# Moving the ReLU tiles by 128 bytes in SBUF, and storing the last two output blocks in halves from two queues

## Chip, cores and metric

The kernel runs on one core of one Trainium2 chip. The metric is the device time of one launch in microseconds; the number that stands for a kernel is the median over its runs.

## The reference

A gated linear attention recurrence is followed by a mixture of four dense experts. Per batch (4) and head (8), over 768 steps of width 48:

```python
state = alpha[:, :, t, :, None] * state + np.einsum('bhd,bhe->bhde', k[:, :, t], v[:, :, t])
y[:, :, t] = np.einsum('bhd,bhde->bhe', q[:, :, t], state)
```

The heads are laid side by side, so that x has 3072 rows of 384. Then, with p the row-normalised domain probabilities, four experts of hidden width 1024:

```python
h = np.maximum(x @ w1[e], 0.0)
out += p[:, e:e + 1] * (h @ w2[e])
```

All inputs and the output are float32.

## The kernel before, in words

**Blocks and groups.** The 3072 rows are 24 blocks of 128 rows, ordered by chunk of the sequence and then by batch. They form seven groups: the first two blocks, then five groups of four, then the last two blocks (`groups`, line 113; `LAST` is the number of the last group). The attention of a block is a generator that is advanced in small steps between matmuls of an earlier group's experts (`advance`, line 728), by due times worked out in `deal` (line 697). The order of the instructions on each engine is the order in which the program issues them; nothing reorders them.

**Tasks.** A task is one expert for one group. Groups before the last two take the four experts in turn. The last two groups go through the experts together: for each expert first group `LAST - 1` (four blocks), then group `LAST` (two blocks) (line 116).

**The two matmul stages.** `up` (line 518) computes the hidden values, eight chunks of 128 for up to 512 rows. From the second group on it does so in three products of split operands (lines 553 to 559), two into the PSUM tile `one` and one into `two`. ScalarE and VectorE then join them in the work tile `t` (lines 568 and 570), ScalarE writes the ReLU (line 595), and VectorE writes two more parts of it (lines 597 and 603). These three parts are the tiles called `hT`: four buffers of 12,288 bytes per partition in the pool `hid`. `down` (line 610) multiplies them by w2: at line 650 an `hT` block of 128 x 128 is the stationary operand (the weight load, LDWEIGHTS, engine PEld), and 384 columns of w2 are the moving operand. While the first groups run, the `hT` buffers are also where w2 is landed by DMA (line 217) and, at the start, the inputs of the second block.

**The output.** `add_up` (line 667) adds a finished PSUM sum to the block's accumulator on VectorE (line 679). The accumulator is the tile `acc` of the pool `hid`, also four buffers; in the last group it is a work tile, `QT`. After the last expert a store of the block's 128 rows of 384 (192 KB) is put on a list (line 686). The list is issued in the next `up`, at the end of its second chunk, and once more at the very end of the program. Stores of the last two groups go on SyncE's queue, all others on GpSimd's.

**Memory.** Pools take space in SBUF in the order in which they are opened, and tiles within a pool in the order of their first use. In the pool `work` the tile `x_raw` (line 455, 6,144 bytes per partition) comes last, and the pool `hid` follows it. In the program before, `x_raw` starts at byte 165,856 of each partition, the four `hT` buffers at 172,000, 184,288, 196,576 and 208,864, and the four `acc` buffers at 221,152 and on. The tiles `t` and `QT` lie before `x_raw`, and the pool with the weights before the whole pool `work`.

Of the kernel before, what the change touches and what calls it, by code (L numbers as in the profile page):

```python
# [10 lines left out]
F32 = mybir.dt.float32  # L11
# [9 lines left out]
def kernel(  # L21
# [37 lines left out]
    nc = tc.nc  # L59
# [3 lines left out]
    P = 128  # L63
# [5 lines left out]
    KC = DM // P  # L69
    FCH = F // P  # L70
    NT = B * P
# [6 lines left out]
    assert DM % P == 0 and F % (P * NQ) == 0 and DM <= 512 and KC * QF == FPQ * DM  # L78
    FINE = 1 + 1 / 4096
    TRIM = 1 - 1 / 8192  # L80

    j = np.arange(P)[:, None] % HALF
    n = np.arange(QUAD)[None, :]
# [7 lines left out]
    work = ctx.enter_context(tc.tile_pool(name="work", bufs=2))  # L91
# [22 lines left out]
    LAST = len(groups) - 1  # L114
# [20 lines left out]
    xraws = {}  # L135
# [4 lines left out]
    stores = deque()  # L140
# [80 lines left out]
    def split_piece(l, i):  # L221
# [3 lines left out]

        nc.scalar.activation(out=top, in_=whole, func=ACT.Copy, scale=TRIM)
        yield
        nc.scalar.activation(out=dif, in_=whole, func=ACT.Copy, scale=TRIM * 4096)
        yield
# [43 lines left out]
    def attention(u):  # L273
# [140 lines left out]
        for s in range(2):  # L414
            rows = slice(HALF * s, HALF * (s + 1))
            nc.scalar.copy(out=parts[:HALF, :, s, :, HALF:], in_=far[rows])
        yield
        for s in range(2):
            rows = slice(HALF * s, HALF * (s + 1))
# [9 lines left out]
        def result():  # L429
            yps = ps.tile([P, KC, P], F32, name="yps", tag="w")  # L430
            for c in range(KC):


                if c < 2:
                    now = [[(2 * c + j // 2, j % 2, (0, HD + TAIL)[j % 2], 2 * QUAD * (j % 2))
                            for j in range(4)]]
                    turns = ([(True, now[0])] if cb > 0 else []) + [(False, now[0])]
                else:
                    turns = [(True, [(p, 0, 0, QUAD) for p in range(NP)])] if cb > 0 else []
                    turns += [(False, [(p, i, QUAD + TAIL * i, 0) for p in range(NP)]) for i in range(2)]  # L440
                for n, (past, turn) in enumerate(turns):
                    for j, (p, i, in_v, in_st) in enumerate(turn):
                        nc.tensor.matmul(  # L443
                            yps[QUAD * j:QUAD * (j + 1), c, :],
                            lhsT=flat_st[:, p, in_st:in_st + QUAD] if past
                            else flat_v[:, p, in_v:in_v + QUAD],
                            rhs=QT[:, p, :] if past else lat[:, 2 * p + i, :],
                            start=(n == 0), stop=(n == len(turns) - 1))
            gi, slot = place[cb, b]
            if slot == 0:  # L450
                if gi == 0:
                    xTs[gi] = work.tile([P, 3, KC, NT], F32R, name="xT", bufs=1)
                    xraws[gi] = xTs[gi][:, 2].bitcast(F32)
                elif gi < LAST:
                    xraws[gi] = work.tile([P, KC, NT], F32, name="x_raw", bufs=1)
                else:
                    xraws[gi] = []
            if gi < LAST:
                nc.scalar.copy(out=xraws[gi][:, :, slot * P:(slot + 1) * P], in_=yps)
            else:  # L460

                xraws[gi].append(AT)
                nc.scalar.copy(out=AT[:, :KC, :], in_=yps)
# [6 lines left out]
        for step in (turn_keys, result) if u >= half else (result, turn_keys):  # L470
            step()
            yield

        if cb < NCB - 1:
# [5 lines left out]
            for i in range(2):  # L480
                rows = slice(HD * i, HD * (i + 1))
# [17 lines left out]
    def split_x(gi, step):  # L499
# [7 lines left out]
        for kc in range(KC) if step == 0 else [step - 1]:  # L507
# [3 lines left out]
            for x, out in pieces:  # L511
                if step == 0:
                    nc.scalar.activation(out=out[0], in_=x, func=ACT.Copy, scale=TRIM)
                else:
# [78 lines left out]
    def hidden_parts(x, parts):  # L593
        top, low, dif = parts
        nc.scalar.activation(out=top, in_=x, func=ACT.Relu, scale=TRIM)  # L595
        yield
# [13 lines left out]
    def down(gi, e, slots, between):  # L610
# [20 lines left out]
        for n, (side, slot, part, fc) in enumerate(steps):  # L631
            c, f = divmod(fc, FPQ)
            advance(cost(1, gi, e) * len(slots) / len(steps))
            while between and n >= between[0][0] * len(steps):
                between.popleft()[1]()
            if n and n % (len(steps) // (2 * len(slots))) == 0:
                background()
            if later and n % (len(steps) // 12 - 1) == len(steps) // 12 - 2:
                make_dif(*later.popleft())
            at = (side, slot)  # L640
            if n == begins[at]:
                sums[at] = ps.tile([P, DM], F32, name="ops", tag="g", bufs=4)
            h = hidden[c][:, :, f, slot * P:(slot + 1) * P]
            if part < 3:
                w = wt[1][first + c].rearrange("p t (c d) -> p t c d", d=DM)[:, part, f]
                h = h[:, part]
            else:
                w = wt[1][first + c].rearrange("p (c d) -> p c d", d=DM)[:, f]
                h = h[:, 2].bitcast(F32)
            nc.tensor.matmul(sums[at], lhsT=h, rhs=w, start=(n == begins[at]), stop=(n == ends[at]))  # L650
            if n == ends[at]:
                add_up(gi, e, slot, side, sums.pop(at))
# [14 lines left out]
    def add_up(gi, e, slot, kind, part):  # L667

        cb, b = groups[gi][slot]
        at = b * NCB + cb  # L670
        if e == 0 and (kind == 0 or not split2(gi, e)):
            accs[cb, b] = hid.tile([P, DM], F32, name="acc", bufs=B) if gi < LAST else \
                work.tile([P, NP * P], F32, name="QT")[:, :DM]
        acc = accs[cb, b]
        scale = (p_fine if kind == 0 else p_all)[:, at, e:e + 1]
        if e == 0 and (kind == 0 or not split2(gi, e)):
            nc.scalar.activation(out=acc, in_=part, func=ACT.Copy, scale=scale)
        else:
            nc.vector.scalar_tensor_tensor(out=acc, in0=part, scalar=scale, in1=acc,  # L679
                                           op0=ALU.mult, op1=ALU.add)  # L680
        if kind == 0:
            return
        if e == E - 1:
            del accs[cb, b]
            row = b * S + cb * P
            stores.append(lambda: (nc.sync if gi >= LAST - 1 else nc.gpsimd).dma_start(
                out=out[row:row + P, :], in_=acc))

# [140 lines left out]
```

## Time and profile before

| what | value |
|---|---|
| median of 6 runs | 1057.86 us |
| lowest and highest run | 1057.08 and 1059.69 us |
| the profiled execution: time | 1059.09 us |
| the profiled execution: span from first to last instruction | 1057.3 us |
| TensorE clock granted | 1.000 over the span |
| DMA: mean rate | 238 GB/s, 251.66 MB |
| stores `out_dram<-acc` from GpSimd's queue | 18 of 192 KB, 6.9 us to landing (median) |
| stores `out_dram<-acc` from SyncE's queue | 4 of 192 KB |
| stores `out_dram<-QT` from SyncE's queue | 2 of 192 KB |

The profile is of one execution. PE is TensorE's matrix multiplication and PEld its weight loads, which overlap it; DVE is VectorE, ACT ScalarE, POOL GpSimd, SP SyncE; a q behind a name means the engine's instruction queue, where DMAs are issued and semaphores waited for. Matmul ends are modelled, so the busy time of one matmul overlaps that of the next; the pace of matmuls is better read from their starts. L650 is line 650 of the kernel.

### The profile page before, as it was taken

The numbers are of one execution on the slowest core, as the hardware profiler recorded it, in microseconds if no ns is written. First come the engines' busy times: TensorE is split into PE (matmuls) and PEld (weight loads), VectorE is DVE, ScalarE is ACT, GpSimd is POOL, SyncE is SP. The second block draws the span as 40 slices with busy tenths as digits, with TensorE's granted clock in tenths as the row PEclk, the third lists the DMA queues.
The fourth block names the chain that finished last, engine by engine and source line by source line (L and its number), as shares of the span: only waits on it lengthen the run. The fifth ranks groups of instructions, "written<-read, shape, count | busy, mean of one in ns | idle before, by whom it ended". The sixth has DMA issues, their size and how long they took to land.

```text
span 1057.3 us, 21578 instructions
## 1 busy us (share of the span) xinstructions
PE 1038.0 (98%) x8498; PEld 903.5 (85%) x8498; DVE 781.7 (74%) x1620; ACT 565.7 (53%) x1195; POOL 35.6 (3%) x77
## 2 busy tenths in 40 slices
PE   8899999999999999999999999999999999999998
PEld 8777777687887899898898898998989989898988
DVE  5578777668779778778877777986877875656565
ACT  4687876575665654545546436555474443323232
POOL 3000010000001000000000000000000000000000
PEclk9999999999999999999999999999999999999999
DMA  7596799997878956757759559586594454444531
GB/s 116 163 340 214 233 305 352 323 338 239 278 265 298 370 195 233 315 169 280 284 176 344 224 174 348 180 287 242 168 372 179 184 210 167 192 183 176 206 153 46
DMA packets 158837, 251.66 MB, mean 238 GB/s; under 512 B 120112, under 2 KB 135344, under 8 KB 136208
## 3 DMA queue, kind: packets, MB, share of 16 engines
q1 hardware_dynamic: 152688, 208.87, 57.8%
q0 software_dynamic: 5760, 41.29, 9.7%
q8 instruction: 67, 1.10, 0.4%
q14 instruction: 34, 0.28, 0.1%
q10 hardware_dynamic: 288, 0.12, 0.1%
HBM read 207.79 MB, written 42.47 MB: 237 GB/s over the span
## 4 chain that ended last, share of the span: by engine, by line
PE 83%; ACT 4%; DVE 4%; DMA 4%; SPq 3%; issue 1%; POOL 0%; ACTq 0%; DVEq 0%; POOLq 0%
PE ops L650 35%; PE one L557 23%; PE two L557 11%; PE sc L348 5%; PE yps L443 3%; PE tp L270 3%; PE one L549 1%; ACT qb L321 1%; SPq L214 1%; PE sps L478 1%; PE far L403 1%; DMA w<-kept 1%; DMA kept<-w 1%; DMA w<-in_moe_w_dram 1%; SPq L215 1%
## 5 line engine op out<-in xcount | busy, mean ns | idle before, releaser
L650 PE MATMUL ops<-w,hT 128*128 128x384 f32 x1872 | 346.9, 340 | 0.2 <-DVE hT L603 0.2
L650 PEld LDWEIGHTS ops<-w,hT 128*128 128x128 f32 x1872 | 324.9, 188 | 4.7 <-ACT t L568 0.6
L557 PE MATMUL one<-xT,w 128*128 128x512 f32 x960 | 252.8, 399 | 1.9 <-DMA w<-kept 1.1
L557 PEld LDWEIGHTS one<-xT,w 128*128 128x128 f32 x960 | 175.7, 188 | 40.6 <-DVE dot L292 1.7
L568 ACT ACTIVATE t<-one 128x512 f32<-128x512 f32 (+1 forms) x192 | 107.1, 558 | 176.2 <-PE one L557 170.9
L321 ACT COPY qb<-QT 64x256 f32<-64x256 f32 x336 | 136.6, 407 | 74.5 <-DVE QT L300 40.9
L597 DVE SCALAR_TENSOR_TENSOR hT<-t,hT 128x512 fp32r<-128x512 f32 (+1 forms) x172 | 110.5, 643 | 68.2 <-ACT hT L595 65.8
L570 DVE TENSOR_TENSOR t<-t,two 128x512 f32<-128x512 f32 (+1 forms) x172 | 109.4, 636 | 57.8 <-ACT t L568 29.1
L595 ACT ACTIVATE hT<-t 128x512 fp32r<-128x512 f32 (+1 forms) x172 | 101.8, 592 | 85.7 <-DVE t L570 84.7
L557 PE MATMUL two<-xT,w 128*128 128x512 f32 x480 | 136.3, 392 | 0.0
L557 PEld LDWEIGHTS two<-xT,w 128*128 128x128 f32 x480 | 90.1, 188 | 20.1 <-DVE acc L679 0.3
L603 DVE SCALAR_TENSOR_TENSOR hT<-hT 128x512 fp32r<-128x512 f32 (+1 forms) x172 | 100.9, 634 | 0.0
L650 PE MATMUL ops<-hT 128*128 128x384 f32 x288 | 100.6, 491 | 0.0
L358 DVE COPY_PREDICATED near<-masks,sc 128x256 f32<-128x256 uint8 x144 | 77.0, 534 | 19.3 <-PE sc L348 16.3
L328 DVE TENSOR_TENSOR QT<-QT,dec 128x256 f32<-128x256 f32 x144 | 61.1, 424 | 35.5 <-ACT qb L321 34.8
L348 PEld LDWEIGHTS sc<-qb,KT 128*64 128x64 f32 x2304 | 72.7, 138 | 9.3 <-issue 4.7
L348 PE MATMUL sc<-qb,KT 128*64 128x64 f32 x2304 | 77.2, 223 | 2.6 <-ACT qb L321 2.6
L650 PEld LDWEIGHTS ops<-hT 128*128 128x128 f32 x288 | 52.1, 190 | 29.0 <-issue 0.4
L679 DVE SCALAR_TENSOR_TENSOR acc<-ops,p_all,acc 128x384 f32<-128x384 f32 x82 | 49.9, 614 | 29.5 <-PE ops L650 28.4
L341 DVE TENSOR_TENSOR KT<-KT,dec 128x256 f32<-128x256 f32 x144 | 60.1, 417 | 0.0
L340 ACT COPY KT<-KT 128x256 f32<-128x256 f32 x138 | 57.5, 416 | 3.0
L549 PE MATMUL one<-xT,w 128*128 128x256 f32 (+1 forms) x240 | 46.8, 341 | 1.8 <-DMA w<-in_moe_w_dram 1.2
(90 smaller groups left out, 933.5 us busy)
## 6 DMA issues: line engine op xcount, KB each, us to landing
w<-kept SPq DMA_DIRECT2D x144, 1152.0 KB
kept<-w POOLq DMA_DIRECT2D x32, 1152.0 KB, 7.7
hT<-in_moe_w_dram SPq DMA_DIRECT2D x32, 384.0 KB
w<-in_moe_w_dram SPq DMA_DIRECT2D x48, 128.0 KB
ra<-in_alpha_dram SPq DMA_DIRECT2D x23, 192.0 KB
rk<-in_k_dram SPq DMA_DIRECT2D x23, 192.0 KB
rq<-in_q_dram SPq DMA_DIRECT2D x23, 192.0 KB
out_dram<-acc POOLq DMA_DIRECT2D x18, 192.0 KB, 6.9
```

Source lines behind the costliest of these rows:

```text
L321: nc.scalar.copy(out=qb[rows, :, i, :].rearrange("p a (b r) -> p a b r", r=m), in_=qv[rows])
L328: nc.vector.tensor_mul(qv, qv, spread(dv[:, :, :, 0], m))
L341: nc.vector.tensor_mul(new[:, :, :, 0, :], old[:, :, :, 0, :], spread(halved(decs[li])[:, :, :, 1], m))
L348: nc.tensor.matmul(out[HALF * s:HALF * (s + 1), 2 * p:2 * p + 2, :], lhsT=KTs[li][:, p, HALF * s:HALF * (s + 1)], rhs=qbs[li][:, p, :, QUA ...
L358: nc.vector.copy_predicated(near.rearrange("p a (b two r) -> p a b two r", two=2, r=m)[:, :, :, 1, :], mk.unsqueeze(1).broadcast_to([P, H, ...
L557: nc.tensor.matmul(out, lhsT=w[:, part, kc], rhs=x_part(gi, part, kc), start=(part == terms[0] and kc == 0), stop=(part == terms[-1] and k ...
L568: nc.scalar.activation(out=t, in_=one, func=ACT.Copy, scale=FINE)
L570: nc.vector.tensor_add(t, t, two)
L595: nc.scalar.activation(out=top, in_=x, func=ACT.Relu, scale=TRIM)
L597: nc.vector.scalar_tensor_tensor(out=low, in0=x, scalar=0.0, in1=top.bitcast(F32), op0=ALU.max, op1=ALU.subtract)
L603: nc.vector.scalar_tensor_tensor(out=dif, in0=top.bitcast(F32), scalar=1 / 4096.0, in1=low.bitcast(F32), op0=ALU.mult, op1=ALU.subtract)
L650: nc.tensor.matmul(sums[at], lhsT=h, rhs=w, start=(n == begins[at]), stop=(n == ends[at]))
```

## The change

Three things are edited. A tile of 32 more floats per partition is allocated for `x_raw`, and only its first 1,536 floats are used; with this, everything in the pool `hid`, that is the `hT` and `acc` buffers, starts 128 bytes further on. The stores of group `LAST - 1` go on GpSimd's queue, as those of the groups before do. The stores of group `LAST` are split into rows 0 to 63 on SyncE's queue and rows 64 to 127 on ScalarE's.

```diff
+    PAD = 32
...
                 elif gi < LAST:
-                    xraws[gi] = work.tile([P, KC, NT], F32, name="x_raw", bufs=1)
+                    xraws[gi] = work.tile([P, KC * NT + PAD], F32, name="x_raw", bufs=1)[:, :KC * NT]
+                    xraws[gi] = xraws[gi].rearrange("p (c n) -> p c n", n=NT)
...
         if e == E - 1:
             del accs[cb, b]
             row = b * S + cb * P
-            stores.append(lambda: (nc.sync if gi >= LAST - 1 else nc.gpsimd).dma_start(
-                out=out[row:row + P, :], in_=acc))
+            queues = (nc.sync, nc.scalar) if gi == LAST else (nc.gpsimd,)
+            for i, queue in enumerate(queues):
+                rows = slice(P // len(queues) * i, P // len(queues) * (i + 1))
+                stores.append(lambda queue=queue, rows=rows: queue.dma_start(
+                    out=out[row:row + P, :][rows], in_=acc[rows]))
```

## The prediction

> **What bounds the kernel now.** I read the page's first part and then the busy time by stage.
>
> ```profile
> span 1057.3 us, 21578 instructions
> ...
> PE 1038.0 (98%) x8498; PEld 903.5 (85%) x8498; DVE 781.7 (74%) x1620; ACT 565.7 (53%) x1195; POOL 35.6 (3%) x77
> ...
> 0.00:60.00 60.00, 52.95 (x600) 45.46 (x602) 35.61 (x89) 36.38 (x86) 10.46 (x30) 1.00 0.73 167
> 60.00:165.00 105.00, 97.59 (x967) 74.97 (x962) 84.32 (x187) 78.69 (x175) 6.93 (x13) 1.00 0.83 276
> 165.00:600.00 435.00, 434.38 (x3512) 369.86 (x3512) 334.99 (x683) 248.83 (x513) 13.94 (x26) 1.00 0.76 271
> 600.00:860.00 260.00, 259.62 (x2323) 231.73 (x2322) 205.94 (x426) 137.96 (x294) 4.31 (x8) 1.00 0.69 248
> 860.00:1036.00 176.00, 176.00 (x991) 164.68 (x990) 109.03 (x209) 57.50 (x116) 0.00 (x0) 1.00 0.43 168
> 1036.00:1057.30 21.30, 17.45 (x120) 16.80 (x119) 11.82 (x29) 6.30 (x16) 0.00 (x0) 1.00 0.11 38
> ```
>
> The stage rows give length, then busy time (and count) of PE, PEld, DVE, ACT and POOL, then clock, DMA share and GB/s. From 165 us to 1036 us PE is busy for 870.0 of 871 us. All its waits after 165 us are these, 2.2 us together:
>
> ```profile
> PE one L557 <- DMA w<-kept: 1.1, 1, 1.1
> PE one L557 <- DVE xT L252: 0.5, 1, 0.5
> PE one L557 <- ACT t L568: 0.4, 1, 0.4
> PE ops L650 <- DVE hT L603: 0.2, 1, 0.2
> ```
>
> So in this stretch only two things change the time: how much matmul work there is, which the edit leaves alone, and the distance from one matmul to the next. I looked at that distance next, because the moved `hT` tiles are the stationary operand of L650. The last expert stages of group `LAST - 1` are four equal stretches of 96 matmuls (start, length):
>
> ```profile
> 866.36 17.12 PE L650 MATMUL ops<-w,hT 128*128 128x384 f32 x96
> ...
> 917.25 16.81 PE L650 MATMUL ops<-w,hT 128*128 128x384 f32 x96
> ...
> 967.84 16.81 PE L650 MATMUL ops<-w,hT 128*128 128x384 f32 x96
> ...
> 1018.88 17.12 PE L650 MATMUL ops<-w,hT 128*128 128x384 f32 x96
> ```
>
> Less the last matmul's own 0.34 us (335 ns, the median of L650), over 95 distances, that is 16.78/95 = 176.6 ns in two of them and 16.47/95 = 173.4 ns in the other two. The program has a slow and a fast pace for the same work on the same buffers. Over the whole trace the 1,730 directly following pairs of L650 that are under 250 ns apart have a mean of 174.7 ns.
>
> **The change, part by part.** *The 128 bytes.* No instruction is added or removed. Moved are `hT` and `acc`. What touches them: L650's 2,160 weight loads, L595, L597 and L603 (172 each), L679, the DMAs that land w2 in `hT`, and the stores of `acc`. First, the engines off PE. The rows that allow a comparison are VectorE's at 512 elements: L597 with both inputs in SBUF takes 694 ns, L603 with both in `hT` 683 ns, L570 with one input in PSUM and nothing in `hT` 685 ns. If a better place of `hT` took L597 down to L603, DVE would gain 11 ns x 140 = 1.5 us; if a worse place did the same the other way to both, it would lose 3.1 us. DVE is 74% busy and PE waited for `hT` 0.2 us after 165 us, so either sits beside PE's work; without that cover it would cost those 1.5 or 3.1 us. L595 (632 ns) is the same as L607 (632 ns), which works in place in `hT`, so there is no ACT penalty for either start.
>
> Second, PE. L650's matmuls start on average 174.7 ns apart with 384 columns. L557, whose stationary operand is w1 and not `hT`, is 120 ns apart with 256 columns and 229 ns with 512, which puts 384 columns at 174.5 ns. A load of `hT` therefore costs the pace nothing today. It also has room: L557 shows a load every 120 ns, L650 needs one every 174. Sorting L650's pairs by which quarter of a 2,048-byte row of `hT` the block begins in, the medians are 174, 174, 175 and 174 ns, and no trend. All four of these starts are 480 bytes past a multiple of 512, though, and after the change all are 96 past one, so this trace cannot show the new place itself. I bound it by the two paces: all 1,872 at 173.4 ns gives (174.7 - 173.4) x 1,872 = -2.4 us; all at 176.6 ns gives +3.6 us. I take 0, because slow and fast stretches read the very same addresses, so something other than the place of `hT` picks the pace. The DMAs that land w2 in `hT` (32 of 384 KB) are issued ahead of use; the largest single PE wait on any DMA after 165 us is the 1.1 us above, on weights that do not move. Bounds 0 and 1.1 us, taken 0.
>
> *Group LAST - 1's four stores, SP to POOL.* On SP they are issued at 1032.44 to 1036.68 us and behind them stand only the two last stores. On POOL nothing is queued at that time (no POOL work after 860 us). The price is in these rows (min/median/max ns, first and last start):
>
> ```profile
> L686 POOL DMA_DIRECT2D out_dram<-acc x18: 539/542/547, 167.6 to 850.4; - x18
> ...
> L686 SPq DMA_DIRECT2D out_dram<-acc x4: 332/334/337, 1032.4 to 1036.7; - x4
> ...
> L826 POOLq DRAIN  x3: 40/93/11434, 850.4 to 1057.1; - x3
> ```
>
> Each issue takes 0.54 instead of 0.33 us. The last is issued at 1036.68, over at 1037.2, and landed 9.3 us later at worst (the maximum of the 18), at 1046.5. POOL's closing drain, 11.4 us after its last store in this trace, would end near 1048.7. The program's end collects the engines at 1056.5 us, so 7.8 us of cover remain: cost 0.
>
> *The last group's stores in halves.* The first block's store (1052.75) lies under the second block's matmuls. The second sets the end: accumulator ready 1054.11, issue at 1054.14 for 0.33 us, first packet 1054.97, last packet over at 1055.64, last landing 1055.99, end of span 1057.32. That is 0.03 + 0.33 + 0.50 + 0.67 + 0.35 + 1.33 = 3.2 us. Only two terms can move. The issue becomes two at once, the one on ACT by its rows (0.39 and 0.45 us at the program's start) up to 0.12 us longer than SP's 0.33; ACT's last work ended at 1047.0, so nothing is behind it but its drain. The 0.67 us of packets for 144 packets become two times 72: -0.33 us if they run side by side without hindrance, 0 if they share the same rate. Bounds -0.34 and +0.12 us. I take -0.1, the middle. The Trainium skill speaks against a gain: "DMA: Bandwidth & Descriptors", section "Rules for kernel authors", says that two transfers to disjoint partition halves serialize on the same engines and one 128-partition transfer is to be used. By that rule the packets stay at 0.67 us and the part costs 0.06 to 0.12 us instead of winning 0.1; no row of this trace has two half stores at once.
>
> **Sum.** 0 + 0 - 0.1 us. Against the profiled execution: 1059.09 - 0.1 = 1059.0 us (span 1057.3 to 1057.2, and 1.8 us around it). The median of the runs is 1.2 us below that execution, so 1057.86 - 0.1 = 1057.8 us.
>
> **The rivals.** *A, the new place holds PE at the fast pace (faster).* For it: two paces exist, and L650 has 1,872 matmuls. Against: they occur on the same addresses. Price -2.4 us, and -0.1 from the tail: 1055.4 us. Should the pace carry over into L557 (mean 229.7, best stretches 229.0 ns, 1,440 matmuls) another -0.9: 1054.4 us.
>
> *B, the new place holds PE at the slow pace (slower).* The weight load of `hT` now meets the moving read of w2 in a worse phase. It decides as soon as the mean distance grows by 1 ns: 1,872 x 1 ns = 1.9 us, about the smallest difference that counts; at 176.6 ns it is +3.6 - 0.1: 1061.4 us. For and against as in A.
>
> *C, GpSimd closes late (slower).* If a POOL store or the drain behind it took longer than 1056.5 - 1037.2 = 19.3 us, each us more would lengthen the end by one. At twice the 11.4 us seen, 1037.2 + 22.9 = 1060.1, +3.5 us: 1061.3 us. The DMA share there is 0.11 against 0.69 in the stage where 11.4 us were seen, so I think it most unlikely.
>
> *D, the place does not change* because `hid` does not follow `x_raw`: then only the tail is left, the forecast's own time.
>
> **How the numbers follow.** Forecast, with D: 0.50. A: 0.26. B: 0.22. C: 0.02. A difference counts from 0.2% on (2.1 us), about what a measurement of this kernel can tell from no change: its six runs spread over 2.6 us. A counts as faster, B and C as slower. So faster 0.26, same 0.50, slower 0.24. The forecast's own range is 1057.8 with the tail's and the DMA's bounds and the runs' scatter, 1056.6 to 1059.5 us. As A and B hold nearly half, the range reaches to both: 1054.4 (A with L557) to 1062.0 us (B with half a us of scatter).
>
> **What would show it.** L650's pairs at a mean of 174.7 ns again, stretches of both 16.81 and 17.12 us: the place does nothing. All stretches alike: A or B. L597 and L603 other than 694 and 683 ns: the place matters to VectorE. The end: two issues near the accumulator's last write, packets over in less than 0.67 us, and 3.1 us from there to the end of the span. POOL's drain over by 1050 us: C is out. The prediction is wrong if PE's busy time between 165 and 1036 us changes by over 2 us with the same number of matmuls.

## The result, and the profile after

| | before | after |
|---|---|---|
| median | 1058.05 us (36 runs) | 1055.52 us (16 runs) |
| lowest and highest run | 1056.64 and 1061.71 us | 1054.42 and 1060.00 us |
| the profiled execution: time and span | 1059.09 and 1057.3 us | 1054.98 and 1053.2 us |
| ratio of the times, 95% interval | | 0.9976 [0.9970, 0.9983] |

The kernel became 0.24% faster, 2.5 us. That is the place and the size of rival A (1055.4 us), not of the forecast (1057.8 us). In the changed file some lines stand further down: L650 is now L653, L557 is L560, L597 is L600, L603 is L606, L679 is L682, L686 is L693, L826 is L833. They shift in the other kernels too; the text keeps to L650 and L557.

The page of the kernel after, and its busy time by stage (columns as before: length; PE, PEld, DVE, ACT, POOL with counts; clock, DMA share, GB/s):

```profile
span 1053.2 us, 21582 instructions
...
PE 1035.7 (98%) x8498; PEld 901.6 (86%) x8498; DVE 781.5 (74%) x1620; ACT 565.3 (54%) x1195; POOL 37.8 (4%) x81
...
165.00:600.00 435.00, 434.32 (x3517) 369.69 (x3516) 335.97 (x684) 249.81 (x516) 13.94 (x26) 1.00 0.77 271
600.00:860.00 260.00, 259.62 (x2325) 231.54 (x2325) 205.88 (x426) 137.30 (x292) 4.30 (x8) 1.00 0.69 247
860.00:1036.00 176.00, 176.00 (x1013) 165.53 (x1012) 109.30 (x212) 57.89 (x119) 2.17 (x4) 1.00 0.42 166
```

PE is as busy as before, 869.9 of 871 us, with the same 8,498 matmuls and the same clock. What differs is how many matmuls fit: 1,013 instead of 991 in the last of these stages. Part of the 22 is that the stage begins earlier in the work, so it is the pace that has to be read. The four equal stretches of 96 matmuls, from the timeline of PE (start, length):

```profile
863.07 16.80 PE L653 MATMUL ops<-w,hT 128*128 128x384 f32 x96
...
913.67 16.80 PE L653 MATMUL ops<-w,hT 128*128 128x384 f32 x96
...
964.26 16.80 PE L653 MATMUL ops<-w,hT 128*128 128x384 f32 x96
...
1014.85 16.80 PE L653 MATMUL ops<-w,hT 128*128 128x384 f32 x96
```

Before, two of the four took 17.12 us; now none does. (16.80 - 0.34)/95 is 173.3 ns from start to start. Over the 1,730 directly following pairs the mean fell from 174.74 to 173.27 ns. All waits of PE after 165 us are 1.1 us together, all for the same releasers as before; of before's list only the 1.1 us for a DMA is missing:

```profile
PE one L560 <- DVE xT L254: 0.5, 1, 0.5
PE one L560 <- ACT t L571: 0.4, 1, 0.4
PE ops L653 <- DVE hT L606: 0.2, 1, 0.2
```

**Where the time went.** The two traces hold the same 8,498 matmuls in the same order, so each start can be set against its counterpart. The span is 4.1 us shorter (1057.3 - 1053.2), more than the medians differ, because the profiled execution of before was 1.0 us above its median and that of after 0.5 us below its own. The 4.1 us are:

| part | after less before |
|---|---|
| waits and small differences up to 175 us | -1.6 us |
| L650's pairs: -1.11 us in 165 to 600, -0.64 in 600 to 860, -0.82 later | -2.57 us |
| L557's pairs | about -0.4 us |
| the steps from one line to another after 175 us | +0.2 us |
| from the last accumulator write to the end | +0.2 us |

The first row does not belong to the edit: three kernels below whose times equal before's (`e2`, `e4`, `e5`) show 1.0 to 1.3 us of it too. Without it, -2.57 - 0.4 + 0.2 + 0.2 = -2.6 us stand beside the 2.5 us of the medians. The share of L557 need not belong to the edit either: `e4`, whose operands stand to each other as before's do, has -0.3 us of it in the same stretch after 1,000 us.

### The profile page after: what moved, and what is told of

The parts are those of the page before. It is cut to its first block, busy times and chain, and to the rows that moved or that the text cites. A ratio compares the mean times of both kernels' runs of the same rounds, so it can differ in the third digit from the quotient of the medians.

```text
span 1053.2 us, 21582 instructions
## 1 busy us (share of the span) xinstructions
PE 1035.7 (98%) x8498; PEld 901.6 (86%) x8498; DVE 781.5 (74%) x1620; ACT 565.3 (54%) x1195; POOL 37.8 (4%) x81
## 4 chain that ended last, share of the span: by engine, by line
PE 86%; DVE 4%; ACT 4%; DMA 3%; SPq 1%; issue 1%; POOL 0%; ACTq 0%; DVEq 0%; POOLq 0%
PE ops L653 36%; PE one L560 23%; PE two L560 11%; PE sc L350 6%; PE yps L445 3%; PE tp L272 3%; DMA hT<-in_moe_w_dram 2%; PE one L552 1%; ACT qb L323 1%; PE sps L481 1%; PE far L405 1%; SPq L216 1%; DMA w<-in_moe_w_dram 1%; DVE w L232 1%; DVE near L360 1%
## 5 line engine op out<-in xcount | busy, mean ns | idle before, releaser
L653 PE MATMUL ops<-w,hT 128*128 128x384 f32 x1872 | 344.4, 340 | 0.2 <-DVE hT L606 0.2
L653 PEld LDWEIGHTS ops<-w,hT 128*128 128x128 f32 x1872 | 322.5, 188 | 4.7 <-ACT t L571 0.6
L560 PE MATMUL one<-xT,w 128*128 128x512 f32 x960 | 252.4, 398 | 0.9 <-DVE xT L254 0.5
L560 PEld LDWEIGHTS one<-xT,w 128*128 128x128 f32 x960 | 175.7, 188 | 39.2 <-ACT t L571 1.4
L600 DVE SCALAR_TENSOR_TENSOR hT<-t,hT 128x512 fp32r<-128x512 f32 (+1 forms) x172 | 110.5, 643 | 68.0 <-ACT hT L598 65.9
L560 PE MATMUL two<-xT,w 128*128 128x512 f32 x480 | 136.2, 392 | 0.0
L560 PEld LDWEIGHTS two<-xT,w 128*128 128x128 f32 x480 | 90.0, 188 | 20.1 <-DVE acc L682 0.6
L653 PE MATMUL ops<-hT 128*128 128x384 f32 x288 | 100.9, 491 | 0.5 <-DMA hT<-in_moe_w_dram 0.5
L606 DVE SCALAR_TENSOR_TENSOR hT<-hT 128x512 fp32r<-128x512 f32 (+1 forms) x172 | 100.9, 634 | 0.0
L653 PEld LDWEIGHTS ops<-hT 128*128 128x128 f32 x288 | 52.1, 190 | 29.8 <-DMA hT<-in_moe_w_dram 1.1
L682 DVE SCALAR_TENSOR_TENSOR acc<-ops,p_all,acc 128x384 f32<-128x384 f32 x82 | 49.8, 614 | 28.7 <-PE ops L653 27.7
```

The lines of the kernel that those rows point to most:

```text
L560: nc.tensor.matmul(out, lhsT=w[:, part, kc], rhs=x_part(gi, part, kc), start=(part == terms[0] and kc == 0), stop=(part == terms[-1] and k ...
L600: nc.vector.scalar_tensor_tensor(out=low, in0=x, scalar=0.0, in1=top.bitcast(F32), op0=ALU.max, op1=ALU.subtract)
L606: nc.vector.scalar_tensor_tensor(out=dif, in0=top.bitcast(F32), scalar=1 / 4096.0, in1=low.bitcast(F32), op0=ALU.mult, op1=ALU.subtract)
```

## The experiments

The theory (T) after the result: the weight load of `hT` and the moving read of w2 go on at the same time, and the pace depends on how the two addresses stand to each other. I count this as the **distance**: the byte address of the stationary operand less that of the moving one, modulo 256. It is 64 for L650 before and 192 after; L557 (stationary w1, moving `xT`) has 192 in both. Rivals: the stores made it (S); the place of `hT` by itself counts, whatever w2's is (P); any other place of `hT` would do (O). In the diffs, 32 floats are 128 bytes.

**1. Each part alone, and two other ways to move.** `e1_pad_only` has the 128 bytes and the old stores, `e2_stores_only` the new stores and the old place. `e4_pad_256B` moves `hT` by 256 bytes, so the distance is again 64. `e5_all_moved` moves everything behind the tile `ident`, weights too: `hT` lies at the addresses of `e1`, and the distance is still 64.

```diff
e1, e4 (with + 64):
-                    xraws[gi] = work.tile([P, KC, NT], F32, name="x_raw", bufs=1)
+                    xraws[gi] = work.tile([P, KC * NT + 32], F32, name="x_raw", bufs=1)[:, :KC * NT]
+                    xraws[gi] = xraws[gi].rearrange("p (c n) -> p c n", n=NT)
e5:
-    ident_all = const.tile([P, P + HALF], F32, name="ident")
+    ident_all = const.tile([P, P + HALF + 32], F32, name="ident")[:, :P + HALF]
```

> The 128 bytes alone, all stores as before. If the place of hT holds L650 at its fast pace: mean distance of directly following L650 matmuls 173.3 ns (after: 173.3, before: 174.7), ratio to before 0.9975 or a little lower, as the tail is 0.2 us shorter than in the changed kernel. If the gain came from the stores: 174.7 ns and ratio 1.000. If the pace is a matter of chance in each program: any mean from 173.3 to 176.7 ns.

> The stores alone, hT in its old place. Place theory: L650 mean 174.7 ns as before, with stretches of both paces, and the end 0.2 us later than before: ratio 1.0002, inside 0.999 to 1.001. Store theory: ratio 0.9975. As nothing changes before 1030 us, this is also a second look at the old place: if the mean of L650 differs much from 174.7 ns here, the pace is drawn anew in each execution.

> hT 256 bytes further on instead of 128, stores as before; its blocks start 224 bytes past a multiple of 512 (before 480, with 128 bytes 96). If what matters is the place within 256 bytes, this is the old place again: L650 mean 174.7 ns, ratio 1.000. If within 512 bytes or more, or if any move away from the old place helps: 173.3 ns, ratio 0.9975. A third value, up to 176.7 ns (ratio 1.003), would mean that the pace depends on the place in steps not yet seen.

> 128 bytes more behind the first tile in SBUF, so that every later tile moves by 128 bytes, hT to its new place and the weights and the work tiles with it; stores as before. If the absolute place of hT matters: L650 mean 173.3 ns, ratio 0.9975. If its place against w2, the operand that L650 reads at the same time, matters: 174.7 ns, ratio 1.000. L557, whose two operands move together, stays at 229.7 ns by the second and may change by the first.

| kernel | L650's distance, mean pace | time (before: 1058.03, 31 runs) | ratio |
|---|---|---|---|
| `e1_pad_only` | 192, 173.28 ns | 1054.96 us (7 runs) | 0.9974 [0.9964, 0.9985] |
| `e2_stores_only` | 64, 174.88 ns | 1057.62 us (11 runs) | 0.9998 [0.9989, 1.0007] |
| `e4_pad_256B` | 64, 174.74 ns | 1057.96 us (11 runs) | 1.0003 [0.9994, 1.0013] |
| `e5_all_moved` | 64, 174.88 ns | 1057.95 us (12 runs) | 1.0001 [0.9992, 1.0010] |

All four stretches of `e1` take 16.80 us; two of them, and three of the four of `e5`, whose `hT` lies at the same addresses, from the timelines:

```profile
863.95 16.80 PE L651 MATMUL ops<-w,hT 128*128 128x384 f32 x96
...
965.16 16.80 PE L651 MATMUL ops<-w,hT 128*128 128x384 f32 x96
```

```profile
865.25 17.12 PE L650 MATMUL ops<-w,hT 128*128 128x384 f32 x96
...
916.23 16.93 PE L650 MATMUL ops<-w,hT 128*128 128x384 f32 x96
...
1018.30 16.81 PE L650 MATMUL ops<-w,hT 128*128 128x384 f32 x96
```

The 128 bytes alone bring the whole gain and the stores none: S falls. Moving the same tiles by 256 bytes brings nothing, so O falls. The same addresses of `hT` run at 173.3 ns in `e1` and at a mix of paces in `e5`, so P falls. What is left is the place of `hT` against something that did not move in `e1` and moved along in `e5`.

The stretch of 16.93 us is a third pace, (16.93 - 0.34)/95 = 174.6 ns. `e4` has it too, in two of its four stretches, where before has 16.81 us:

```profile
916.51 16.93 PE L651 MATMUL ops<-w,hT 128*128 128x384 f32 x96
```

So a distance of 64 allows three paces, and before's mean of 174.74 ns, which `e4` meets to the digit, is a mix that another execution may make up differently. `e2` shows that the program alone does not choose the pace: up to 1,030 us it has before's instructions at before's addresses, and L650's stretches have before's paces up to 890 us. In the next one, of 46 distances, it has 176.7 ns and before 173.3 ns.

**2. Against what?** `e6_work_moved` leaves the weights and moves the work tiles (`KT`, `t`, `xT`, `x_raw`) and `hT` by 128 bytes, as the two buffers of `AT` grow by 64 bytes each. If `hT`'s partner were a work tile, L650 would go back to 174.7 ns. It also takes L557's distance from 192 to 64.

```diff
-        AT = work.tile([P, NP, P], F32, name="AT")
+        AT = work.tile([P, NP * P + 16], F32, name="AT")[:, :NP * P].rearrange("p (a n) -> p a n", n=P)
```

> 128 bytes more ahead of t, xT, x_raw and hT (two AT tiles grown by 64 bytes each), so that all of these move together against the weights; stores as before. If the partner of hT is w2, which L650 reads at the same time: L650 mean 173.3 ns. If it is a tile that moves along here (t, xT): 174.8 ns. L557 has its operands 128 bytes apart anew too (stationary less moving 64 instead of 192, within 256): if the rule is the same for L557, it goes from 229.6 to a slower mean, up to 233.3 ns, 1,440 x 3.7 ns = 5.3 us, and the kernel is slower than with the 128 bytes alone, ratio between 0.9975 and 1.003.

It took 1060.07 us (12 runs; before 1057.98, 17 runs), ratio 1.0023 [1.0011, 1.0035]: slower, while L650 stayed at 173.37 ns. The partner is no work tile. What became slower is L557, 233.21 instead of 229.65 ns. Nine of its matmuls in the timelines of PE, first after, then `e6`:

```profile
899.25 1.54 PE L560 MATMUL one<-xT,w 128*128 128x512 f32 x6
900.62 0.85 PE L560 MATMUL two<-xT,w 128*128 128x512 f32 x3
901.31 1.54 PE L560 MATMUL one<-xT,w 128*128 128x512 f32 x6
```

```profile
903.60 1.56 PE L557 MATMUL one<-xT,w 128*128 128x512 f32 x6
905.00 0.86 PE L557 MATMUL two<-xT,w 128*128 128x512 f32 x3
905.70 1.56 PE L557 MATMUL one<-xT,w 128*128 128x512 f32 x6
```

From the first start to the third, nine matmuls take 2.06 us (229 ns each) in one and 2.10 us (233 ns) in the other. The second large matmul line has paces that go by distance too. Its 256-column matmuls, those of the last group, show nothing of the kind: their moving operand is `KT`, their distance went from 0 to 128 in `e6`, and the median from start to start from 120 to 119 ns.

**3. Other distances.** Three single runs, with a gap behind the tile `dec6`, which lies just ahead of `xT`, and another in `x_raw` (floats: 16 and 32 in `e7`, 48 and 32 in `e8`, 24 and 0 in `e9`). The rival here was a rule of halves: fast wherever the distance lies in one half of the 256 bytes, from 128 on. The diff is the first part of `e7`; the gap in `x_raw` is made as in `e1`.

```diff
-            dec = work.tile([P, NP, P // (2 * m)], F32, name=f"dec{li}", bufs=1)
+            gap = 16 if li == 6 else 0
+            dec = work.tile([P, NP * P // (2 * m) + gap], F32, name=f"dec{li}", bufs=1)
+            dec = dec[:, :NP * P // (2 * m)].rearrange("p (a n) -> p a n", a=NP)
```

> xT 64 and hT 192 bytes further on, stores as before. Stationary less moving, within 256 bytes: L650 0 (before 64, after 192), L557 128 (before and after 192). If two operands in the same half of 256 bytes are the slow case: L650 174.8 ns, L557 as before at 229.6 ns. If only the distance of 64 is slow: L650 173.3 ns.

> xT 192 and hT 320 bytes further on, stores as before: L650 at a distance of 128, L557 at 0 (within 256 bytes). By halves: L650 173.3 ns, L557 slower than 229.6 ns, up to 233.3. If only a distance of exactly 192 is fast: L650 174.8 ns.

> xT and hT 96 bytes further on, stores as before: L650 at a distance of 160, L557 at 96. By halves: L650 173.3 ns, L557 slower than 229.6 ns. A mean between 173.3 and 174.8 ns would say that the pace falls in steps of 32 bytes and not in two halves.

| kernel | L650: distance, pace | L557: distance, pace | time |
|---|---|---|---|
| `e7_x64_h192` | 0, 173.58 ns | 128, 232.92 ns | 1059.27 us |
| `e8_x192_h320` | 128, 176.03 ns | 0, 228.47 ns | 1058.28 us |
| `e9_x96_h96` | 160, 176.60 ns | 96, 234.08 ns | 1066.30 us |

The rule of halves fails in all three: for L650 it expected 174.8 ns at 0 and 173.3 ns at 128 and 160, for L557 no change at 128 and a slower pace at 0. At distances of 0 and 128 the two lines agree: 0 is a fast place and 128 a slow one for both. In `e9` both are at their slowest, and it is 8.3 us (0.8%) slower than before's 1057.98 with not one instruction more; the highest of before's 17 runs beside it is 1062.22 us. The timeline of `e9`:

```profile
871.63 17.12 PE L652 MATMUL ops<-w,hT 128*128 128x384 f32 x96
```

and all its waits of PE after 165 us are one line:

```profile
PE one L559 <- DVE xT L252: 0.3, 1, 0.3
```

PE waits less than in any other kernel here, 0.3 us, and the kernel is the slowest. A list of waits says nothing about pace.

**4. Finer, and the best of each.** `f1` and `f2`, single runs, put both lines at 224 and both at 32 (gaps of 56 and 48, 40 and 16 floats). `f3` joins the best measured ones, L650 at 192 and L557 at 0 (48 and 48 floats), with the old stores.

> xT and hT placed so that L650 and L557 both have their two operands at a distance (stationary less moving, within 256 bytes) of 224, stores as before. Seen so far: L650 174.8 ns at 64, 173.3 at 192, 173.6 at 0, 176.0 at 128, 176.6 at 160; L557 228.5 at 0, 233 at 64 to 128, 229.5 at 192. If the pace is a function of the distance that runs on between these: L650 from 173.3 to 173.6 ns, L557 from 228.5 to 229.5 ns or lower. A value far outside says that neighbours in 32 bytes have nothing to do with each other.

> The same with both distances at 32, stores as before. If the pace runs on between its neighbours 0 and 64: L650 from 173.6 to 174.8 ns, L557 from 228.5 to 233.2 ns.

> xT 192 and hT 384 bytes further on, stores as before: the best distance seen for each line, L557 at 0 and L650 at 192. If the distance within 256 bytes is all that counts, for each line by itself: L650 173.3 ns and L557 228.5 ns, which against the 128 bytes alone is 1,440 x 0.9 ns = 1.3 us less, ratio to before 0.9962 (0.995 to 0.9975). If the two lines disturb each other, L557 stays near 229.4 ns and the ratio at 0.9975.

| kernel | L650: distance, pace | L557: distance, pace | time |
|---|---|---|---|
| `f1_both_224` | 224, 175.25 ns | 224, 233.22 ns | 1063.35 us |
| `f2_both_32` | 32, 173.85 ns | 32, 232.99 ns | 1061.12 us |
| `f3_x0_h192` | 192, 173.34 ns | 0, 228.67 ns | 1054.08 us (5 runs) |

`f1` missed its expectation on both lines: between two good places, 192 and 0, lies a worse one. For L650 its mean is a mix again: the stretches of `f1` run at 173.3 or at 176.7 ns, so that 64 and 224 allow a slow pace beside the fast one, where at the other five distances L650's stretches of over 40 matmuls stay within 1 ns of one another. At 32 the two lines do not agree: it is a fast place for L650 and a slow one for L557. That ends any reading between measured points, or from one line to another. The paces have to be measured, at steps of 32 bytes at least. `f3` has the lowest time: 1054.08 us against 1058.57 (8 runs) beside it, ratio 0.9961 [0.9947, 0.9975]. In its timeline nine matmuls of L557 take 2.05 us:

```profile
900.40 1.52 PE L560 MATMUL one<-xT,w 128*128 128x512 f32 x6
901.76 0.84 PE L560 MATMUL two<-xT,w 128*128 128x512 f32 x3
902.45 1.52 PE L560 MATMUL one<-xT,w 128*128 128x512 f32 x6
```

Whether it beats the changed kernel is not settled by times, as the intervals of the two ratios overlap and the runs are of different series.

**5. Is w2 the partner?** `g1_w2_alone` moves w2 by 128 bytes and all that lies behind it, `hT` too, by 256. Counted modulo 256 only w2 has moved, so that L650's distance goes to 192 and L557's stays.

```diff
+    ahead_gap = const.tile([P, 32], F32, name="ahead_gap")
...
+        behind_gap = wts.tile([P, 32], F32, name="behind_gap", bufs=1)
+        for t in (ahead_gap, behind_gap):
+            nc.gpsimd.memset(t, 0.0)
```

> w2 moved instead of hT: 128 bytes more ahead of the w2 tiles and 128 more behind them, so that w2 lies 128 bytes further on and everything after it 256; within 256 bytes only w2 has a new place, and L650's distance (stationary less moving) goes from 64 to 192, L557's stays at 192. Stores as before; two small memsets on GpSimd are added at the start. If w2 is the partner of hT and only their distance within 256 bytes counts: L650 173.3 ns, L557 229.3 to 229.8 ns, ratio 0.9975. If hT's place against some other tile counts: L650 174.8 ns, ratio 1.000.

It took 1057.93 us (11 runs; before 1057.93, 15 runs), ratio 1.0008 [0.9998, 1.0019]. The time missed its expectation; the pace of L650 met it, 173.26 ns and four stretches of 16.80 us:

```profile
864.89 16.80 PE L651 MATMUL ops<-w,hT 128*128 128x384 f32 x96
...
966.70 16.80 PE L651 MATMUL ops<-w,hT 128*128 128x384 f32 x96
```

So with `hT` 256 bytes on, which by itself left the mix of paces (`e4`), 128 bytes on w2 bring the fast pace: w2 is the partner. What took back most of the gain is L557, at an unchanged distance of 192: 230.74 instead of 229.65 ns, 1.6 us by 1,440 matmuls. From `g1`'s timeline:

```profile
899.00 1.56 PE L558 MATMUL one<-xT,w 128*128 128x512 f32 x6
900.40 0.86 PE L558 MATMUL two<-xT,w 128*128 128x512 f32 x3
901.10 1.56 PE L558 MATMUL one<-xT,w 128*128 128x512 f32 x6
```

That is 2.10 us for nine, as in `e6`. The mean distance of L557's pairs in the stretches that hold over 40 of them with no break of 1 us, in order of time (ns, worked out from the starts):

```
before  229.0 229.1 229.0 228.9 229.0 229.4 229.2 228.9 228.9 233.3
after   229.0 229.1 229.0 229.0 229.0 229.0 229.5 229.0 229.0 229.0
e2      229.1 231.6 229.0 228.9 229.0 229.4 229.1 233.3 229.0 228.9
g1      229.1 231.6 231.6 231.9 231.6 230.7 229.5 233.3 233.3 233.3
f3      227.7 228.6 228.7 228.3 228.6 228.6 227.7 227.2 227.2 227.2
```

At a distance of 192, L557 has two paces, 229.0 and 233.3 ns, as L650 has several at 64, and falls into the one or the other by stretches. In before one of the ten is slow. In `g1` three are slow throughout, and the five from 230.7 to 231.9 ns begin at the slow pace and go over to the fast one where a few other matmuls come between. What picks the pace is open, and so is why `g1` picks the slow one so often.

**All kernels by one sum.** With 1,872 matmuls of L650 and 1,440 of L557, and before's 174.74 and 229.65 ns at 1058.05 us, the two measured paces of a kernel give its time:

| kernel | by the paces | measured |
|---|---|---|
| after | 1054.9 us | 1055.52 us |
| `e1` | 1054.9 | 1054.96 |
| `e2`, `e4`, `e5` | 1058.5, 1057.8, 1058.4 | 1057.62, 1057.96, 1057.95 |
| `e6` | 1060.6 | 1060.07 |
| `e7`, `e8`, `e9` | 1060.6, 1058.8, 1067.9 | 1059.27, 1058.28, 1066.30 |
| `f1`, `f2` | 1064.1, 1061.2 | 1063.35, 1061.12 |
| `f3` | 1054.0 | 1054.08 |
| `g1` | 1056.8 | 1057.93 |

For `e6`, as an example: 1,872 x (173.37 - 174.74) ns = -2.6 us and 1,440 x (233.21 - 229.65) ns = +5.1 us, so 1058.05 + 2.6. Over a range of 12 us the sum is right to 1.6 us, with the paces of one trace of each kernel; the largest misses are `e9`, `e7` and `g1`. What else changed in them is worth no more than these misses. Part of `g1`'s 1.1 us lies at the start, where two memsets were added: up to 175 us its trace is 0.4 us shorter than before's, those of `e2`, `e4` and `e5` are 1.0 to 1.3 us shorter.

## Why the prediction was right or wrong

- **What bounds the kernel: right.** PE without waits, and so only the pace counts. The gain is pace. PE's busy time between 165 and 1036 us could not show it, though it was named as the sign of being wrong: an engine that is busy throughout fills a fixed window at any pace, 870 us before and after. The sign that did show it is the other one, all stretches alike.
- **The 128 bytes on PE: the step that failed.** "I take 0, because slow and fast stretches read the very same addresses, so something other than the place of `hT` picks the pace." The first half is true, the conclusion does not follow. The place of `hT` against w2 decides which paces exist at all (at 192 only 173.3 ns, at 64 also 174.6 and 176.6); where there are several, something else picks one. The trace had shown that a second pace exists at the old place; it could not show that it exists at every place. The bound was right: -2.4 us by 1,872 distances at 173.4 ns, -2.57 us measured.
- **Rival A happened**, close to its price (1055.4 against 1055.52 us), in part by luck: the price had the tail at -0.1 us, and it was +0.2. The range of 1054.4 to 1062.0 us holds the result only because it was stretched to the rivals; the forecast's own, 1056.6 to 1059.5, does not. The pace did not carry over into L557, whose addresses kept their distance: -0.4 us, with -0.3 of it in `e4` too, where I gave -0.9 for a complete carry-over.
- **"A load of `hT` therefore costs the pace nothing today"** was wrong. I compared L650 with L557 (174.7 by 174.5 ns) and took L557 for a line without trouble. It has operand distances of its own: 0 where I took the 120 ns, 192 where I took the 229. `f3` shows 227.2 ns for 512 columns at 0, and half-way between 120 and 227.2 lies 173.6 ns: L650 was 1.1 ns slower than that.
- **The sorting by quarters of a row** could show no trend: quarters begin 512 bytes apart, and in `e4` 256 bytes more left the mean as it was. The sorting varied what does not matter.
- **VectorE, ACT, and the DMAs into `hT`: right.** The groups of before's 694 and 683 ns are, after:

```profile
L600 DVE SCALAR_TENSOR_TENSOR hT<-t,hT 128x512 fp32r<-128x512 f32 x140 | 97.1, 694 | 67.4 <-ACT hT L598 65.5
...
L606 DVE SCALAR_TENSOR_TENSOR hT<-hT 128x512 fp32r<-128x512 f32 x140 | 89.9, 684 | 0.0
```

- **Stores moved to POOL: right, cost 0, rival C out.** The issues and POOL's closing drain, by form:

```profile
L693 POOL DMA_DIRECT2D out_dram<-acc x22: 539/542/547, 166.5 to 1032.6; - x22
```

```profile
L833 POOLq DRAIN  x3: 40/102/5047, 1032.6 to 1052.9; - x3
```

The drain after the last store ends at 1032.6 + 5.0 = 1037.6 us, over 15 us before the end of the span.

- **Stores in halves: a loss of 0.2 us instead of a gain of 0.1, outside my bounds of -0.34 and +0.12.** Issue of the half stores, by form (min/median/max ns):

```profile
L693 SPq DMA_DIRECT2D out_dram<-QT x2: 512/534/557, 1048.4 to 1049.8; - x2
L693 ACTq DMA_DIRECT2D out_dram<-QT x2: 499/538/577, 1048.4 to 1049.8; - x2
```

From the last accumulator write to the end, before and after: start of issue 0.03 and 0.03 us, issue 0.33 and 0.51, to the first packet 0.50 and 0.65, packets 0.67 and 0.92, to the last landing 0.35 and 0.34, to the end of the span 1.33 and 0.97; together 3.21 and 3.42 us. `e2`, with the same stores, has 3.44, and all twelve kernels with the old stores have 3.21 to 3.23. I had priced the longer issue on ACT alone; the issue was longer on both queues (0.50 to 0.58 us against 0.33). And the packets hardly shared time: ACT's half ran from 1050.97 to 1051.65 us and SP's from 1051.50 to 1051.90, nearly one after the other. That agrees with the rule of the Trainium skill that the prediction weighed against the gain ("DMA: Bandwidth & Descriptors", "Rules for kernel authors"). The estimate of 0.06 to 0.12 us by that rule was nearer than mine, and still too low. Against 1058 us no difference of 0.2 us shows in the times (`e2`).

Still open: by what mechanism inside the chip the place of the two operands acts on the pace, why neighbouring steps of 32 bytes differ as they do, and what picks the pace at a distance that allows several. The period of 256 bytes is seen at two distances of L650: 64 (`e4` against before) and 192 (`f3`, with `hT` moved by 384 bytes, against `e1`).

## What to carry to other kernels

When the busiest engine shows no waits, look at the distance from one start to the next, stretch by stretch: two values for equal work mean there is a pace to be won, and here a change of address won it. Then vary the address of the one operand against that of the other in small steps and measure each, since neither the middle between good places nor an allocation that merely happened to be good can be trusted. Any edit that changes the size of a tile moves all tiles behind it, so a comparison of two kernels within 1% should have the distances of their matmul operands beside it.

## What the runs showed of the hardware

- The pace of this kernel's matmuls that each load new weights depends on where the two operands lie to each other within 256 bytes of a partition: means of 173.3 to 176.6 ns for 384 columns (1.9%), 228.5 to 234.1 ns for 512 (2.5%), and 1054.1 to 1066.3 us for the whole kernel. For 256 columns no loss shows at the two distances that occur (120 ns at 0, 119 ns at 128). The Trainium skill, "TensorE: Matmul & The Clock Gate", section "Part 2: What happens when you issue a matmul", has two independent read ports and says that loading the next weights "doesn't steal SBUF read bandwidth from the running matmul". By that alone the place of the one operand against the other should not count. In the runs, with the same instructions, it does, so the measurement decides; in what way the two reads meet, no run shows.
- A pace, once settled, holds for as long as one line's matmuls follow each other unbroken; where it changed (173.3 and 176.7 ns for L650, 229.0 and 233.3 ns for L557), other matmuls had come between. In the settled stretches the distances repeat: 173, 173, 174 ns in the fast one of L650, and sequences such as 178, 175, 178, 176, 177, 176 ns in the slow one; 226, 229, 232 ns or 233, 233, 234 ns in L557 at 192, and 226, 227, 227 ns at 0.
- Two stores of 64 rows, begun on SP and ACT within 5 ns, took 0.50 to 0.58 us to issue on each queue; one store of 128 rows on SP took 0.33 us. Whether the fewer rows or the second issue beside it makes it longer, no run shows.
